# Attention, soft mixture and dense block in one kernel: a weight load moved eight pairs later, diagonals moved ahead of outputs, combining moved to VectorE and partly into the dense stage

## The chip, the cores and the metric

The kernel runs on one core of a Trainium2 chip. The metric is the device time of one execution in microseconds (us), lower is better. The engines are PE (TensorE matmul; PEld is its weight load), DVE (VectorE), ACT (ScalarE), POOL (GpSimd) and SP (SyncE, which here issues every DMA).

## What is computed

Three layers follow each other. The first is linear attention with a decaying state over 4 batches, 8 heads, 768 tokens and 48 dimensions per head. The second is a soft mixture of 8 experts with 4 slots each. The third is a dense block with a gelu between two matrices.

```python
# attention, per batch and head, t = 0..767
y[t] = r[t] @ (state + outer(u * k[t], v[t]))
state = w[t][:, None] * state + outer(k[t], v[t])
# soft mixture: x is (3072, 384), phi (384, 32)
logits = x @ phi
d = softmax(logits, axis=0); slot_input = d.T @ x
slot_out[e] = relu(slot_input[e] @ w1[e]) @ w2[e]      # 8 experts, hidden size 1024
c = softmax(logits, axis=1); x = c @ slot_out
# dense block: w_in (384, 2048), w_out (2048, 384)
h = x @ w_in
out = (h * sigmoid(1.702 * h)) @ w_out
```

`w_in` and `w_out` arrive as 64-bit floats and are turned into 32-bit floats on the chip with integer operations.

## The kernel before, in words

The program has three stages, and the order of the instructions of each engine is the order in which the code is written (`tc.manual_schedule()`).

**The pair loop** (`phase_a`, the loop over `i` at L650). Two heads form a pair, so there are 16 pairs, four to a batch. Iteration `i` works on pair `i` (`cur`), prepares pair `i+1` (`nxt`) and ends pair `i-1` (`prv`). For each pair DVE scans the decays (`products`, L498 and L501), multiplies keys and queries by them (`scale`, L507) and scans the states (L552). ACT makes six diagonal matrices for each half of a pair, `diagonal(i, 0)` and `diagonal(i, 3)` (L534, tile `am`, three buffers). `causal` (L568, DVE) puts PE's scores beside them in `am`. `outputs(i-1, c0)` (PE, L579 and L584) uses `am`, the values `v` and the states, and ends with a copy on ACT to `xt` (L587). `x_tr` (L600) transposes `xt` on PE, ACT copies the result (L601), and `logits` (L811) multiplies `xt` by phi.

The loads go out on SP in the order of the code and wait there until their buffers are free: the decays `z` (L466), keys and queries `rk` (L473), values `v` (L480, two buffers, wanted by `states`, L549, of the next iteration), one 512 KB piece of the first half of `w_in` (L114) in each of the iterations 1 to 6, and one or two 512 KB pieces of the expert weights w1 (L79).

**Combining** (`Batch.combining`, L887). The softmax over the 32 slots of a batch's tokens: DVE subtracts the maximum, ACT takes the exponential, DVE sums and inverts; then ACT multiplies six column groups by the inverse (L901, six instructions) and rounds (L902), DVE takes the rest of the rounding (L908, twice), and POOL copies the rounded half twice (L909). `combined` (L912) transposes the result on PE, three 128x128 blocks for each half of a batch (L917), and ACT copies it to the token buffer `cT`. Batches 0 and 1 are combined in the last iteration, batches 2 and 3 in the expert stage (`phase_b`).

**The expert stage** (`phase_b`). PE multiplies the slot inputs by w1 (L988, four groups of 24), ACT takes the relu (L1009), PE transposes (L1017), DVE copies into `hTm` (L1019, which POOL has set to zero, L999), and PE multiplies by w2 (L1025, 128 instructions). Beside it DVE and ACT turn the six pieces of `w_in` into 32-bit floats (`step`, L290 to L303). Loads of w2 and `w_out` start as each group of L988 frees its buffers (`W.turn`).

**The dense stage** (`phase_c`, loop over `n` at L1235, 96 steps). Each step has one matmul with the combined table (`act`, L1108), a gelu and a rounding on ACT (L1115, L1122), the rest of the rounding on DVE (`low`, L1130, tile `gl`), and nine matmuls (`project`, L1146). Conversions of `w_out` and of the late half of `w_in` run beside it on DVE and ACT. Steps 16 to 23 work on token block 2, steps 24 to 31 on block 3.

Of the kernel before, what the change touches and what calls it, by code (L numbers as in the profile page):

```python
# [27 lines left out]
NS = 32  # L28
# [179 lines left out]
def body(ctx, tc, rkz, z0, vin, vt, wc, uin, phi, w1, w2, w_in, w_out, cst, out):  # L208
# [22 lines left out]
    with ExitStack() as c1:  # L231
        wip = c1.enter_context(tc.tile_pool(name="wip", bufs=1, reuse_waits="tile"))
        ring = c1.enter_context(tc.tile_pool(name="ring", bufs=1, reuse_waits="tile"))
        with tc.manual_schedule(), ExitStack() as c2:
            W = Weights(tc, ring, wip, w1, w2, w_in, w_out)
            short = ExitStack()
            batches, sp, sT = phase_a(tc, rkz, z0, vin, u_sb, prod, ebias, W, c2, short, consts, soft)
            dense = phase_b(tc, W, c2, short, sp, sT, soft, batches, ebias)
            phase_c(tc, W, c2, dense, ebias, soft, out,
                    Check(tc, wc, prod, con, flag, peak))  # L240
# [178 lines left out]
def phase_a(tc, rkz, z0, vin, u_sb, prod, ebias, W, after, late, consts, soft):  # L419
# [5 lines left out]
    with ExitStack() as ctx:  # L425
# [224 lines left out]
        for i in range(n_p + 1):  # L650
# [52 lines left out]
            if cur and i:  # L703
                diagonal(i, 3)
# [8 lines left out]
            if 0 < i <= KT * HF // CV:  # L713
                W.load_in(i - 1)
# [57 lines left out]
class Tokens:  # L772
# [25 lines left out]
class Batch:  # L798
# [88 lines left out]
    def combining(self, room):  # L887

        nc, pool = self.tc.nc, self.pool
        cc, chl = [t.rearrange("p (c s) -> p c s", c=6) for t in halves(room())]  # L890
        mx = pool.tile([128, 6], F32, name="mx", bufs=2)
        nc.vector.tensor_reduce(out=mx, in_=self.l, axis=AX.X, op=ALU.max)
        nc.vector.tensor_tensor(out=cc, in0=self.l, in1=mx.unsqueeze(2).to_broadcast([128, 6, NS]), op=ALU.subtract)
        nc.scalar.activation(cc, cc, AF.Exp)
        yield
        sm = pool.tile([128, 6], F32, name="sm", bufs=2)
        nc.vector.tensor_reduce(out=sm, in_=cc, axis=AX.X, op=ALU.add)
        nc.vector.tensor_scalar_add(sm, sm, 1e-9)
        nc.vector.reciprocal(sm, sm)
        for c in range(6):  # L900
            nc.scalar.mul(cc[:, c], cc[:, c], sm[:, c:c + 1])  # L901
        nc.scalar.copy(chl.bitcast(F32R), cc)  # L902
        yield
        self.c4 = []
        for h in range(2):
            c4 = room().rearrange("p (c a s) -> p c a s", c=3, a=4)
            hi2, cc2 = [t[:, 3 * h:3 * h + 3].unsqueeze(2).to_broadcast([128, 3, 2, NS]) for t in (chl, cc)]
# [14 lines left out]


def halves(t):
    return t[:, 0:6 * NS], t[:, 6 * NS:]
# [9 lines left out]
def phase_b(tc, W, after, late, sp, sT, soft, batches=(), ebias=None):  # L935
# [6 lines left out]
    with late:  # L942
# [9 lines left out]
        step = W.in_steps(ebias, {0: flat, 1: flat, 4: h[:, 512:]}) if batches else lambda *a: None  # L952
# [18 lines left out]
        def combine(b):  # L971
            for bt in batches[b:b + 1]:
                for i in range(2):
                    pct = bt.combined(i, bt.psT.tile())
                    nc.scalar.copy(bt.home(i), pct)

        c2, c3 = [bt.combining(room) for bt in batches[2:]] if batches else (iter(()),) * 2
        next(c2, None)
        step(0, 0)
        step(0, 1)  # L980
        next(c2, None)
        step(0, 2)
        ph = psH.tile([128, 512], F32, name="ps")
        for n, p in enumerate((3, 0, 1, 2)):
# [5 lines left out]
            if n == 0:  # L990
                next(c2, None)
                step(1, 0)
                step(1, 1)
            if n == 1 and batches:
                cT.room(1, F32R)
                combine(2)
                next(c3, None)
                step(1, 2)
                nc.gpsimd.memset(hTm, 0.0)  # L999
                next(c3, None)  # L1000
                step(2, 0)
                step(2, 1)
            W.turn(n)
        next(c3, None)
        step(2, 2)
        if not batches:
            nc.gpsimd.memset(hTm, 0.0)
        for q in range(2):
            nc.scalar.activation(h[:, 256 * q:256 * q + 256], ph[:, 256 * q:256 * q + 256], AF.Relu)  # L1009
        tiny = bp.tile([128, 1], F32, name="tiny")  # L1010
        nc.scalar.activation(tiny, h[:, 0:1], AF.Gelu_apprx_sigmoid)
        combine(3)
# [9 lines left out]
        for e in range(NE):  # L1022
# [11 lines left out]
            for m, i in (((3, 0), (3, 1), (4, 0)), ((4, 1), (3, 2), (5, 0)), ((5, 1), (4, 2)), ((5, 2),))[e] if e < 4 else ():  # L1034
                step(m, i)
# [3 lines left out]
    return cvp, room, psA, mid, psH, psS, po, rep  # L1039


def phase_c(tc, W, after, dense, ebias, soft, out, check=None):
    nc = tc.nc
    con, cT = soft[0], soft[3]
    cvp, room, psA, mid, psH, psS, po, rep = dense
    with ExitStack() as c2:
# [188 lines left out]
        for n in range(1, n_all):  # L1235
# [86 lines left out]
```

## Time and profile before

| | us |
|---|---|
| three runs | 443.34, 444.67, 446.39 |
| median | 444.67 |
| the profiled execution | 444.18 |
| its span, first to last instruction | 442.3 |
| busy in the span: PE, DVE, ACT, POOL | 406.4, 323.0, 265.4, 50.6 |

The mean granted clock of TensorE over the span is 0.967 of full speed. The profile is one execution, recorded by the hardware. A row of a timeline gives the start and the length in us, the engine, the line, the operation and the tiles, and in brackets the idle time just before it and who ended that.

### The profile page before, as it was taken

The page shows a single profiled execution, that of the slowest core. Times are in us where ns is not written, and L with a number is a line of the kernel's source. Part 1 is how long each engine was busy: PE and PEld are TensorE (multiplying, and loading weights), DVE is VectorE, ACT ScalarE, POOL GpSimd, SP SyncE. Part 2 cuts the span into 40 slices and gives each one's busy share as a digit, 9 for nine tenths or more (in the row PEclk, how much of TensorE's full clock was granted, in tenths as well). Part 3 has the DMA queues.
Part 4 walks back from the last instruction along what each step waited for, and adds up shares of the span by engine and source line. Part 5 has one row for each costly group of instructions (what it writes and reads, how often), then busy time and mean ns, then how long its engine had stood idle before and what let it go on. Part 6 is the DMA issues. An engine that isn't in the chain of part 4 may idle for free.

```text
span 442.3 us, 8909 instructions
## 1 busy us (share of the span) xinstructions
PE 406.4 (92%) x3405; PEld 310.7 (70%) x3405; DVE 323.0 (73%) x522; ACT 265.4 (60%) x647; POOL 50.6 (11%) x82
## 2 busy tenths in 40 slices
PE   5887989899999978799999999999999999999993
PEld 1565667667767655295788788877888888888872
DVE  7799599899999755896995888587763765644431
ACT  5476567677777865544875657486565544445530
POOL 4323132222322310220000000000000000000000
PEclk9599699999999998989999999999999999999997
DMA  8969699998785886999500000000000634401102
GB/s 210 225 153 303 182 306 266 243 239 248 192 226 139 317 292 258 368 414 424 240 1 0 0 2 1 1 0 1 18 0 2 185 107 137 142 19 72 71 3 79
DMA packets 24565, 67.35 MB, mean 152 GB/s; under 512 B 2848, under 2 KB 6560, under 8 KB 24256
## 3 DMA queue, kind: packets, MB, share of 16 engines
q1 hardware_dynamic: 24512, 66.67, 48.2%
q8 instruction: 29, 0.48, 0.4%
q14 instruction: 24, 0.20, 0.1%
HBM read 61.94 MB, written 4.72 MB: 151 GB/s over the span
## 4 chain that ended last, share of the span: by engine, by line
PE 65%; DMA 13%; DVE 11%; ACT 5%; issue 2%; POOL 1%; SPq 1%; DVEq 0%; ACTq 0%; POOLq 0%
PE po L1146 43%; DMA v<-in_vin 7%; PE pa L1108 5%; DMA wt<-in_rkz 5%; PE py L584 3%; PE py L579 3%; PE ps L1025 2%; ACT am L534 2%; PE pkv L549 2%; PE pg L562 2%; DMA wt<-in_w_in 2%; DVE wt L498 1%; DVE wt L507 1%; PE ps L600 1%; ACT c L901 1%
## 5 line engine op out<-in xcount | busy, mean ns | idle before, releaser
L1122 ACT CAST gh<-g 128x512 fp32r<-128x512 f32 x96 | 59.4, 619 | 62.5 <-PE po L1146 62.1
L1130 DVE TENSOR_TENSOR gl<-g,gh 128x512 fp32r<-128x512 f32 x96 | 65.2, 687 | 41.8 <-ACT gh L1122 41.4
L1146 PE MATMUL po<-gh,wi 128*128 128x512 f32 x288 | 88.8, 390 | 0.0
L1146 PE MATMUL po<-gh,wt 128*128 128x512 f32 x288 | 83.8, 390 | 0.0
L534 ACT ACTIVATE am<-con,cT 128x128 f32<-128x128 f32 x192 | 59.4, 392 | 9.7 <-DVE cT L527 9.7
L1146 PEld LDWEIGHTS po<-gh,wt 128*128 128x128 f32 x288 | 54.1, 188 | 11.8 <-issue 0.4
L1146 PEld LDWEIGHTS po<-gh,wi 128*128 128x128 f32 x288 | 54.2, 188 | 11.6
L1115 ACT ACTIVATE g<-pa 128x512 f32<-128x512 f32 x96 | 57.0, 594 | 2.5 <-PE pa L1108 1.9
L1146 PE MATMUL po<-gl,wi 128*128 128x512 f32 x144 | 56.4, 391 | 0.0
L1146 PE MATMUL po<-gl,wt 128*128 128x512 f32 x144 | 51.4, 393 | 1.4 <-DVE gl L1130 1.4
L1108 PE MATMUL pa<-cT,wt 128*128 128x512 f32 x96 | 38.4, 402 | 1.1 <-ACT g L1115 1.1
L568 DVE COPY_PREDICATED am<-con,pg 128x768 f32<-128x768 uint32 x32 | 32.3, 1009 | 7.4 <-ACT am L534 7.3
L1146 PEld LDWEIGHTS po<-gl,wt 128*128 128x128 f32 x144 | 27.0, 188 | 7.9 <-DVE gl L1130 2.2
L587 ACT COPY xt<-py 128x384 f32<-128x384 f32 x32 | 15.2, 480 | 28.1 <-PE py L584 27.0
L1146 PEld LDWEIGHTS po<-gl,wi 128*128 128x128 f32 x144 | 27.0, 188 | 5.7
L492 POOL TENSOR_TENSOR rkb<-wt 128x384 f32<-128x384 f32 x25 | 28.0, 1120 | 17.0 <-DMA wt<-in_rkz 11.9
L501 DVE TENSOR_TENSOR_SCAN wt<-wt 128x774 f32<-128x774 f32 x16 | 28.4, 1772 | 0.5
L579 PE MATMUL py<-am,v 128*64 128x128 f32 x384 | 28.4, 283 | 0.4 <-DVE am L568 0.4
L498 DVE TENSOR_TENSOR_SCAN wt<-wt 128x774 f32<-128x774 f32 (+1 forms) x17 | 28.1, 1658 | 0.3 <-DMA wt<-in_z 0.3
L562 PE MATMUL pg<-wt 64*128 64x128 f32 x312 | 25.7, 300 | 0.5 <-DVE am L568 0.5
L562 PEld LDWEIGHTS pg<-wt 64*128 64x128 f32 x312 | 20.6, 197 | 5.7 <-issue 1.8
L579 PEld LDWEIGHTS py<-am,v 128*64 128x64 f32 x384 | 21.1, 140 | 2.7 <-DVE am L568 0.6
(210 smaller groups left out, 581.5 us busy)
## 6 DMA issues: line engine op xcount, KB each, us to landing
wt<-in_w SPq DMA_DIRECT2D x21, 512.0 KB, 7.0
wt<-in_w SPq DMA_DIRECT2D x13, 768.0 KB, 9.2
wt<-in_rkz SPq DMA_DIRECT2D x26, 288.0 KB, 5.2
v<-in_vin SPq DMA_DIRECT2D x16, 296.0 KB, 5.4
c<-in_wc SPq DMA_DIRECT2D x24, 192.0 KB, 2.9
out_dram<-os SPq DMA_DIRECT2D x18, 256.0 KB, 2.1
wt<-in_rkz SPq DMA_DIRECT2D x30, 145.3 KB, 3.9
wi<-in_w_in SPq DMA_DIRECT2D x6, 512.0 KB, 6.4
```

Of the source, the lines that this page charges most:

```text
L492: eng.tensor_tensor(out=rkb[:, c], in0=st[p]["r"][:, c], in1=st[p]["k"][:, c], op=ALU.mult)
L498: nc.vector.tensor_tensor_scan(out=sf[:, o:n][:, ::-1], data0=z[:, o + 1:n + 1][:, ::-1], data1=dS[:, o:n][:, ::-1], initial=0.0, op0=ALU. ...
L501: nc.vector.tensor_tensor_scan(out=x, data0=z[:, 0:XL], data1=dX, initial=0.0, op0=ALU.mult, op1=ALU.add)
L534: nc.scalar.activation(am[:, j, c], ident, AF.Copy, scale=q["coef"][:, c0 + c, j:j + 1])
L562: nc.tensor.matmul(q["pg"][:, j, (c - c0) * CH:(c - c0 + 1) * CH], q["k"][64 * j:64 * j + 64, c * CH:(c + 1) * CH], q["r"][64 * j:64 * j + ...
L568: nc.vector.copy_predicated(q["am", c0], later, q["pg"][:, :, 0:3 * CH].rearrange("p j (c t) -> p j c t", t=CH))
L579: nc.tensor.matmul(py[64 * j:64 * j + 64, (c - c0) * CH:(c - c0 + 1) * CH], q["v"][:, c * 96 + j * 48:c * 96 + j * 48 + 64], q["am", c0][: ...
L1108: nc.tensor.matmul(pa, mst[:, f * 128:(f + 1) * 128], cT.at(tb * 512, 512), start=True, stop=True)
L1115: nc.scalar.activation(g, live[n], AF.Gelu_apprx_sigmoid)
L1122: nc.scalar.copy(gh, live[n])
L1130: nc.vector.tensor_tensor(out=gl, in0=g, in1=gh.bitcast(F32), op=ALU.subtract)
L1146: nc.tensor.matmul(live["po", tb][i], w[:, i * 128:(i + 1) * 128], g, start=(f % FH == 0 and k == 0), stop=(f % FH == FH - 1 and k == 2))
```

## The change

The change has four parts.

1. The six pieces of `w_in` are loaded in the iterations 8 to 13 in place of 1 to 6.
2. `diagonal(i, 3)` stands ahead of `outputs(i-1, 3)` in place of behind it and `scale`.
3. Combining works in place on the tile `l`. The multiplication by the inverse is one DVE instruction per batch, the rounding two on DVE, and POOL copies half as much (L909 copied both halves of a 4-column layout, the new one copies one).
4. For batches 2 and 3 only the subtraction and the exponential stay in the expert stage. The rest runs in the dense stage, on DVE at steps 17 and 25, with the transposes and copies at steps 20 and 28. In the expert stage the conversion has a room of its own for its second piece, the zeros of `hTm` come from ACT in place of POOL, and the load of the gelu's table stands ahead of the conversions in place of behind the relu.

```diff
@@ phase_a, the loop over i
+            if cur and i:
+                diagonal(i, 3)
             if prv:
                 outputs(i - 1, 3)
...
-            if cur and i:
-                diagonal(i, 3)
...
-            if 0 < i <= KT * HF // CV:
-                W.load_in(i - 1)
+            if n_p // 2 <= i < n_p // 2 + KT * HF // CV:
+                W.load_in(i - n_p // 2)
...
             if i == n_p - 1:
-                for _ in range(2):
-                    for it in comb:
-                        next(it, None)
+                for it in comb:
+                    run(it)
@@ combining
-        for c in range(6):
-            nc.scalar.mul(cc[:, c], cc[:, c], sm[:, c:c + 1])
-        nc.scalar.copy(chl.bitcast(F32R), cc)
-        yield
+        nc.vector.tensor_tensor(out=cc, in0=cc, in1=sm.unsqueeze(2).to_broadcast([128, 6, NS]), op=ALU.mult)
...
-            nc.vector.tensor_tensor(out=c4[:, :, 2:], in0=cc2, in1=hi2, op=ALU.subtract)
-            nc.gpsimd.tensor_copy(c4[:, :, 0:2], hi2)
+            part, hi = cc[:, 3 * h:3 * h + 3], c4[:, :, 0]
+            nc.vector.tensor_copy(hi.bitcast(F32R), part)
+            nc.vector.tensor_tensor(out=c4[:, :, 2:], in0=part.unsqueeze(2).to_broadcast([128, 3, 2, NS]),
+                                    in1=hi.unsqueeze(2).to_broadcast([128, 3, 2, NS]), op=ALU.subtract)
+            nc.gpsimd.tensor_copy(c4[:, :, 1], hi)
@@ phase_b
-        step = W.in_steps(ebias, {0: flat, 1: flat, 4: h[:, 512:]}) if batches else lambda *a: None
+        step = W.in_steps(ebias, {0: flat, 1: flat[:, 1024:], 4: h[:, 512:]}) if batches else lambda *a: None
...
+        comb = [bt.combining(room) for bt in batches[2:]]
+        for it in comb:
+            next(it)
+        nc.scalar.activation(bp.tile([128, 1], F32, name="tiny"), con[:, 0:1], AF.Gelu_apprx_sigmoid)
...
             if n == 0:
                 step(1, 2)
                 step(2, 0)
                 step(2, 1)
+                nc.scalar.copy(hTm, con[:, OFF_MASK:OFF_MASK + 1].unsqueeze(2).to_broadcast([128, HT, NE * 36]))
...
-                combine(2)
...
-                nc.gpsimd.memset(hTm, 0.0)
...
-        combine(3)
@@ phase_c, the loop over n
+            for k, (bt, it) in enumerate(zip(batches[2:], comb)):
+                if n == FH * (k + 2) + 1:
+                    run(it)
+                if n == FH * (k + 2) + 4:
+                    for i in range(2):
+                        nc.scalar.copy(bt.home(i), bt.combined(i, bank(1 - k, i)))
             project(n)
```

On ACT in the pair loop, the end of one iteration and the start of the next stand so before. `am` is the tile of the diagonals, `xt` that of the outputs, `xb` that of the transposed outputs.

```order
L514 COPY prod<-wt_80 128x6
L587 COPY xt<-py 128x384 x2
L534 ACTIVATE am<-con,cT_115 128x128 x6
L601 COPY xb<-ps_365 128x288
L601 COPY xb<-ps_370 128x288
```

And so in the changed kernel:

```order
L514 COPY prod<-wt_80 128x6
L587 COPY xt<-py 128x384
L534 ACTIVATE am<-con,cT_115 128x128 x6
L587 COPY xt<-py 128x384
L601 COPY xb<-ps_364 128x288
L601 COPY xb<-ps_369 128x288
```

The six diagonals of the second half moved ahead of the copy of the second outputs. In the last iteration the same copy (of pair 14) also moved behind them.

On ACT in the expert stage, from the exponential of batch 2 to the last conversion, the order before is this. `c` is a combining tile, `hTm`, `wi` and `wt_88` hold conversions, `wt_88<-ps` is the relu.

```order
L894 ACTIVATE c_2350<-c_2350 128x192
L298 ACTIVATE hTm<-hTm,ebias 128x512
L901 ACTIVATE c_2350<-c_2350,sm 128x32 x6
L902 CAST c_2350<-c_2350 128x192
L298 ACTIVATE hTm<-hTm,ebias 128x512
L975 CAST cT_2410<-ps_2411 128x384
L975 CAST cT_2410<-ps_2416 128x384
L894 ACTIVATE c_2421<-c_2421 128x192
L901 ACTIVATE c_2421<-c_2421,sm 128x32 x6
L902 CAST c_2421<-c_2421 128x192
L298 ACTIVATE wi<-wi,ebias 128x512
L1009 ACTIVATE wt_88<-ps 128x256 x2
```

And in the changed kernel:

```order
L892 ACTIVATE l_2009<-l_2009 128x192
L892 ACTIVATE l_2271<-l_2271 128x192
L967 ACT_TABLE_LOAD
L967 ACTIVATE tiny<-con 128x1
L298 ACTIVATE hTm<-hTm,ebias 128x512 x2
L298 ACTIVATE wi<-wi,ebias 128x512
L984 COPY hTm<-con 128x2304
L992 ACTIVATE wt_88<-ps 128x256 x2
```

Fourteen combining instructions (six multiplications and a rounding for each of two batches) and two copies to `cT` left the way to the relu; a table load, which stood behind the relu, and a copy of 2304 columns came onto it. The line numbers here are those of the changed kernel.

On DVE in the dense stage the changed kernel has this at step 17, between the `gl` of steps 18 and 19, which before stood side by side. `l_2009` is the tile of batch 2's exponentials, `c_3042` and `c_3046` its two halves.

```order
L1111 TENSOR_TENSOR gl<-g,gh 128x512
L895 TENSOR_REDUCE sm<-l_2009 128x6
L896 TENSOR_SCALAR sm<-sm 128x6
L897 RECIPROCAL sm<-sm 128x6
L898 TENSOR_TENSOR l_2009<-l_2009,sm 128x192
L903 CAST c_3042<-l_2009 128x3x32
L904 TENSOR_TENSOR c_3042<-l_2009,c_3042 128x3x64
L903 CAST c_3046<-l_2009 128x3x32
L904 TENSOR_TENSOR c_3046<-l_2009,c_3046 128x3x64
L1111 TENSOR_TENSOR gl<-g,gh 128x512
```

Eight instructions of a batch moved from the expert stage to a place between two products that PE waits for; batch 3 has the same at step 25.

## Rows read from the trace of the kernel before

**Rows 1.** Busy us by window: length, PE, PEld, DVE, ACT, POOL, clock, DMA share, GB/s.

```profile
11.40:150.00 138.60, 125.83 (x1800) 92.99 (x1800) 124.53 (x137) 98.95 (x310) 36.86 (x59) 0.94 0.83 228
173.80:190.50 16.70, 13.99 (x113) 5.85 (x114) 14.38 (x32) 10.12 (x29) 3.81 (x5) 0.92 0.95 364
190.50:213.80 23.30, 22.18 (x199) 16.56 (x199) 19.33 (x40) 10.25 (x21) 2.29 (x3) 0.99 1.02 417
213.80:438.00 224.20, 219.47 (x981) 179.01 (x979) 145.36 (x274) 124.89 (x230) 0.00 (x0) 1.00 0.14 47
```

**Rows 2.** The chain that ended last, in the pair loop: start, us, what.

```profile
37.15 7.69 DMA v<-in_vin
44.97 1.04 PE pkv L549 x20
...
59.44 5.50 DMA v<-in_vin
```

**Rows 3.** Two more windows, columns as in the first group.

```profile
45.00:50.00 5.00, 5.00 (x56) 4.30 (x56) 2.40 (x2) 1.16 (x4) 0.18 (x1) 0.50 0.32 73
...
120.00:140.00 20.00, 19.14 (x296) 14.55 (x296) 18.54 (x20) 14.61 (x46) 5.44 (x9) 1.00 0.59 171
```

**Rows 4.** Timeline of DVE, the first scan of three iterations in a row.

```profile
39.25 1.76 DVE L498 TENSOR_TENSOR_SCAN wt<-wt 128x774 f32<-128x774 f32 x1
...
52.42 1.74 DVE L498 TENSOR_TENSOR_SCAN wt<-wt 128x774 f32<-128x774 f32 x1
...
61.18 1.75 DVE L498 TENSOR_TENSOR_SCAN wt<-wt 128x774 f32<-128x774 f32 x1
```

**Rows 5.** Waits between 30 and 150 us: total us, times, longest.

```profile
ACT xt L587 <- PE py L584: 24.9, 13, 6.3
...
DVE am L568 <- ACT am L534: 3.0, 6, 0.6
```

**Rows 6.** Timeline of PE in the last iteration.

```profile
166.40 0.53 PE L811 MATMUL pl<-xt,phis 128*32 128x192 f32 x8 [1.41 <-ACT xt L587]
```

**Rows 7.** Timeline of the expert stage, single engines.

```profile
179.19 0.96 PE L917 MATMUL ps<-con,c 128*128 128x128 f32 x6
...
183.07 2.02 POOL L999 MEMSET hTm<- 128x2304 f32 x1 [3.52 <-DVE wi L303]
...
183.25 1.87 DVE L898 TENSOR_SCALAR sm<-sm 128x6 f32<-128x6 f32 x1
...
188.00 0.64 ACT L1009 ACTIVATE wt<-ps 128x256 f32<-128x256 f32 x2
...
188.12 1.54 PE L917 MATMUL ps<-con,c 128*128 128x128 f32 x6 [2.68 <-POOL c L909]
...
188.66 1.28 ACT L1011 ACT_TABLE_LOAD   x1
...
189.45 1.06 PE L1017 MATMUL ps<-con,wt 128*128 128x128 f32 x4
...
190.47 4.59 PE L1025 MATMUL ps<-wt,hTm 128*32 128x384 f32 x48
```

**Rows 8.** Timeline of the dense stage, DVE and PE around steps 18 to 21.

```profile
253.14 1.28 DVE L1130 TENSOR_TENSOR gl<-g,gh 128x512 fp32r<-128x512 f32 x2
...
256.53 1.28 DVE L1130 TENSOR_TENSOR gl<-g,gh 128x512 fp32r<-128x512 f32 x2
...
256.32 0.39 PE L1146 MATMUL po<-gl,wt 128*128 128x512 f32 x1
...
258.61 0.39 PE L1146 MATMUL po<-gl,wt 128*128 128x512 f32 x1
```

**Rows 9.** Groups of instructions by line, up to 235 us: busy us, mean ns.

```profile
L908 DVE TENSOR_TENSOR c<-c 128x192 f32<-128x192 f32 x6 | 2.3, 428 | 2.6 <-ACT c L902 2.6
...
L909 POOL COPY c<-c 128x192 f32<-128x192 f32 x6 | 2.7, 484 | 27.3 <-ACT c L902 27.3
...
L1122 ACT CAST gh<-g 128x512 fp32r<-128x512 f32 x13 | 8.0, 616 | 2.2 <-PE po L1146 2.0
```

More of the change, by code (lines that the diff above doesn't have):

```diff
@@ L239, in body @@
             phase_c(tc, W, c2, dense, ebias, soft, out,
-                    Check(tc, wc, prod, con, flag, peak))
+                    Check(tc, wc, prod, con, flag, peak), batches)
     ok = nc.values_load(flag, min_val=0, max_val=NFLAG)
@@ L887, in combining @@
     def combining(self, room):
-        nc, pool = self.tc.nc, self.pool
-        cc, chl = [t.rearrange("p (c s) -> p c s", c=6) for t in halves(room())]
+        nc, pool, cc = self.tc.nc, self.pool, self.l
         mx = pool.tile([128, 6], F32, name="mx", bufs=2)
-        nc.vector.tensor_reduce(out=mx, in_=self.l, axis=AX.X, op=ALU.max)
-        nc.vector.tensor_tensor(out=cc, in0=self.l, in1=mx.unsqueeze(2).to_broadcast([128, 6, NS]), op=ALU.subtract)
+        nc.vector.tensor_reduce(out=mx, in_=cc, axis=AX.X, op=ALU.max)
+        nc.vector.tensor_tensor(out=cc, in0=cc, in1=mx.unsqueeze(2).to_broadcast([128, 6, NS]), op=ALU.subtract)
         nc.scalar.activation(cc, cc, AF.Exp)
@@ L906, in combining @@
             c4 = room().rearrange("p (c a s) -> p c a s", c=3, a=4)
-            hi2, cc2 = [t[:, 3 * h:3 * h + 3].unsqueeze(2).to_broadcast([128, 3, 2, NS]) for t in (chl, cc)]
-            nc.vector.tensor_tensor(out=c4[:, :, 2:], in0=cc2, in1=hi2, op=ALU.subtract)
-            nc.gpsimd.tensor_copy(c4[:, :, 0:2], hi2)
+            part, hi = cc[:, 3 * h:3 * h + 3], c4[:, :, 0]
[3 more added lines that the diff above has]
+            nc.gpsimd.tensor_copy(c4[:, :, 1], hi)
             self.c4.append(c4)
@@ L921, in home @@
         return self.soft[3].at(self.b * S + h * 3 * CH, 3 * CH)
-def halves(t):
-    return t[:, 0:6 * NS], t[:, 6 * NS:]
 def slot_inputs(tc, pool, SI):
@@ L969, in room @@
             return sp.tile([128, 12 * NS], F32, name="c4", bufs=3)
[L971 to L978, printed above, removed]
+        comb = [bt.combining(room) for bt in batches[2:]]
+        for it in comb:
+            next(it)
+        nc.scalar.activation(bp.tile([128, 1], F32, name="tiny"), con[:, 0:1], AF.Gelu_apprx_sigmoid)
         step(0, 0)
         step(0, 1)
-        next(c2, None)
+        step(1, 0)
+        step(1, 1)
         step(0, 2)
@@ L990, in phase_b @@
             if n == 0:
[L991 to L995, printed above, removed]
-                combine(2)
-                next(c3, None)
                 step(1, 2)
-                nc.gpsimd.memset(hTm, 0.0)
-                next(c3, None)
                 step(2, 0)
                 step(2, 1)
+                nc.scalar.copy(hTm, con[:, OFF_MASK:OFF_MASK + 1].unsqueeze(2).to_broadcast([128, HT, NE * 36]))
+            if n == 1:
+                step(2, 2)
+                step(3, 0)
+                if batches:
+                    cT.room(1, F32R)
             W.turn(n)
[L1004 to L1007, printed above, removed]
         for q in range(2):
             nc.scalar.activation(h[:, 256 * q:256 * q + 256], ph[:, 256 * q:256 * q + 256], AF.Relu)
-        tiny = bp.tile([128, 1], F32, name="tiny")
-        nc.scalar.activation(tiny, h[:, 0:1], AF.Gelu_apprx_sigmoid)
-        combine(3)
+        step(3, 1)
         h4 = h[:, 0:512].rearrange("p (q c r) -> p q r c", q=2, r=2)
@@ L1033, in phase_b @@
                                           ident.rearrange("p (n s) -> p n s", n=4).unsqueeze(2).to_broadcast([128, 4, 2, NS]))
-            for m, i in (((3, 0), (3, 1), (4, 0)), ((4, 1), (3, 2), (5, 0)), ((5, 1), (4, 2)), ((5, 2),))[e] if e < 4 else ():
+            for m, i in (((3, 2), (4, 0), (4, 1)), ((5, 0), (5, 1), (4, 2)), ((5, 2),))[e] if e < 3 else ():
                 step(m, i)
@@ L1038, in phase_b, with phase_c @@
                 cvp = after.enter_context(tc.tile_pool(name="cvp", bufs=1, side="right", reuse_waits="tile"))
-    return cvp, room, psA, mid, psH, psS, po, rep
-def phase_c(tc, W, after, dense, ebias, soft, out, check=None):
+    return comb, cvp, room, psA, mid, psH, psS, po, rep
+def phase_c(tc, W, after, dense, ebias, soft, out, check=None, batches=()):
     nc = tc.nc
     con, cT = soft[0], soft[3]
-    cvp, room, psA, mid, psH, psS, po, rep = dense
+    comb, cvp, room, psA, mid, psH, psS, po, rep = dense
     with ExitStack() as c2:
```

## The prediction

> **What bounds the kernel now.** I read the busy times by stage first [rows 1]. The reader is to see three regimes. In the pair loop (138.6 us) PE is busy for 125.83 and DVE for 124.53, so both are near their limit and the time is lost in short waits. In the expert stage (16.7 us) PE has 13.99 and DVE 14.38, and the DMA share is 0.95. In the dense stage PE is busy for 219.47 of 224.20, so every matmul added there costs its full length, and DVE has slack (145.36).
>
> Then I read the chain of waits. In the pair loop one link stands out: the values `v` issued at 37.15 land 7.69 us later, and `states` on PE starts only then, at 44.97 [rows 2]. The next such link takes 5.50. After the wait PE runs at half its clock: the granted clock is 0.50 between 45 and 50 us [rows 3], which is its level of 1.2 GHz. On DVE the first scan of this iteration (iteration 3) stands at 39.25, that of the next at 52.42, the one after at 61.18 [rows 4]. So iteration 3 takes 13.17 us and the next one 8.76.
>
> Then the waits by engine. ACT waits 24.9 us in 13 waits for the second outputs of the pair before, and DVE waits 3.0 us in 6 waits for the diagonals that stand behind that wait on ACT [rows 5]. In the expert stage PE waits 2.68 us for POOL's copy of batch 3's combining weights before it may transpose them, and only behind these does it transpose the relu and start on w2 at 190.47 [rows 7].
>
> All terms are set against the profiled execution, 444.18 us: its span of 442.3 and 1.9 around it. The median of the three runs is 0.5 above it, and I leave that out.
>
> **Part 1, `w_in` eight pairs later.** Six loads of 512 KB move; none is added. When the slow `v` is issued, two of the six are ahead of it or right behind it on SP. Without them its 7.69 us should fall to about the 5.50 of the next link or below, and 2.2 us is most of the wait; the half clock after the wait goes with it. So iteration 3 should take what iteration 4 took, 8.76, although that one had its own piece of `w_in`: 13.17 - 8.76 = 4.4 gained. What is late next is again `v`: its buffer comes free at the end of an iteration, and 5.5 us of landing and the 20 matmuls of `states` follow, which fills the 8.76 us. So nothing below that is to be had from this part.
>
> The pieces now meet iterations 8 to 13, queued behind `v` and ahead of w1, as before. Their price there has two ends. It is nothing where the DMA has room: between 120 and 140 us (iterations 12 and 13) its share is 0.59 [rows 3]. It is 4.4 us for one stall like that of iteration 3. I take 0.5, near the lower end, because iteration 4 shows what a piece costs without the backlog of the start: 8.76 us, no stall. Net of part 1: -3.9.
>
> **Part 2, diagonals ahead of outputs.** On ACT six diagonals now fill the wait for the second outputs, 24.9 / 13 = 1.9 us on average [rows 5]. At most DVE's 3.0 us are gained. The other end is a loss: where ACT comes late, the copy to `xt` slips behind the diagonals, and PE's transposes, which read it, wait. No row shows this; with a slip of 0.5 us in three iterations it is +1.5. I take -1.2, less than half of the 3.0, since in most iterations the `v` link sets the pace [rows 2] and takes back what DVE gains.
>
> In the last iteration the multiplications and roundings of two batches (14 instructions) leave ACT, and with them the wait of 1.41 us that PE has there for the copy of `xt` [rows 6]. Against it, `x_tr` of pair 14 now waits for a copy that stands behind the diagonals, and DVE has six instructions more. Between -1.4 and +0.5 I take -1.2, near the row: PE has other work queued in both orders, and DVE's work is done before the next maximum is asked for.
>
> **Part 3, the expert stage.** PE loses six transposes ahead of its third group, 0.96 us, the wait of 2.68, and six transposes from 188.12 to the relu's transposes at 189.45, 1.33 [rows 7]. The relu, 0.64, lay beside that wait and is now on the path. That is 0.96 + 2.68 + 1.33 - 0.64 = 4.3, and I take 4.0 for new gaps. Its cover is ACT: the zeros for `hTm` stand ahead of the relu. They take between 2.0 us (POOL's time for the same columns [rows 7]) and 2.8 (4.5 times a 512-column rounding of 616 ns [rows 9]). DVE needs 14 instructions before ACT may start on them, at 14.38 / 32 = 0.45 each 6.3 us [rows 1], so until about 180; with a conversion between, ACT is done near 184. PE's first layer ends at 185.44 - 0.96 = 184.5 (before, it ended 2.68 ahead of 188.12). So the zeros just fit. DVE, relieved of ten small instructions and of the 1.87 us below, should have its conversions done before PE is through w2.
>
> One instruction of six columns on DVE took 1.87 us, and it lies within POOL's zeroing of `hTm`, 183.07 to 185.09 [rows 7]. The Trainium skill (SBUF — State Buffer, "Who interferes with whom") says that GpSimd and a VectorE copy, cast or scalar operation in a two-port mode take turns at one shared port pair, each for the whole instruction; the trace agrees. That rule also speaks against the change, which puts two casts per batch on DVE beside POOL's copies; it is a rival below.
>
> The gelu's table load took 1.28 us [rows 7]. It now stands ahead of the first conversion on ACT, where DVE still has four subtractions and the first half of a conversion to do; it costs nothing. The Trainium skill (ScalarE: Activation LUTs, "Rules for kernel authors") budgets about 2.7 us for a switch to another set; by that the zeros would end some 1.4 us later, and the sum would be 438.2 in place of 436.8. The row decides.
>
> **Part 4, the dense stage.** Twelve transposes come to PE. At full clock six took 0.96 us, after the wait 1.54 [rows 7]; between 1.9 and 3.1 for twelve, and I take 1.9, since the clock here is 1.00 [rows 1]. On DVE eight instructions come between two `gl`. The dearest kind took 428 ns [rows 9], so at most 3.4 us per batch; most handle fewer columns, and I take 2.4. The `gl` of step 19 is ready at 254.42 and wanted at 256.32, that of step 20 ready near 257.2 and wanted at 258.61 [rows 8]: 1.9 and 1.4 us of slack. Step 19 becomes 2.4 - 1.9 = 0.5 late. Step 20 is then wanted 0.5 later, and 0.96 more by the transposes ahead of it, so it waits for nothing. That is 0.5 per batch, 1.0 for both; the ends are nothing and 2 x (3.4 - 1.4) = 4.0. ACT's four copies lie in its idle time (124.89 busy of 224.20). Part 4: +2.9.
>
> **Sum.** -3.9 - 1.2 - 1.2 - 4.0 + 2.9 = -7.4, so 444.18 - 7.4 = 436.8.
>
> **Rivals.**
>
> *The stall moves.* `v` of one of the iterations 8 to 11 lands late, because these have all other loads too. For it: the DMA share over the loop is 0.83 [rows 1]. Against it: iteration 4 had a piece and no stall. One stall of 4.4 gives 441.2.
>
> *Loads hold the second layer.* PE comes to w2 four us earlier, but the loads that start with the first layer do not come earlier, and the DMA share is 0.95 and then 1.02 [rows 1]. The price is up to the 4.0 of part 3; half of it gives 438.8.
>
> *The diagonals bring nothing.* The copy of `xt` takes over as what PE waits for. That gives 436.8 + 1.2 = 438.0.
>
> *POOL's copies hold DVE.* A copy of twice the columns took 484 ns [rows 9]; four copies in the dense stage, each holding DVE once, are up to 1.9 us on PE's path, 438.7. This is the port rule of the Trainium skill named above (SBUF — State Buffer).
>
> *Slower.* The loads of iterations 8 to 11 (keys, queries, decays, values, one or two pieces of w1 and now one of `w_in`) fill the queue so that `v` stalls in each as in iteration 3, with the half clock behind it. Four stalls are 17.6 us: 454.4. From three on (436.8 + 13.2 = 450.0) the change is slower by over 1%. Against it stand the iterations 1, 2 and 4 to 6 of before, which had the same loads, and one stall among six.
>
> *More is gained.* All 3.0 us of the diagonals and nothing lost in the later iterations give 436.8 - 1.8 - 0.5 = 434.5, and less with PE at full clock in the second layer.
>
> **How the numbers follow.** A measurement of this kernel can tell about 1% from no change, 4.4 us of the median of 444.67. The forecast (434 to 440) has 0.52, the moved stall 0.17, the held second layer 0.10, idle diagonals 0.06, POOL's copies 0.04, the slower case 0.05, the larger gain 0.06. Faster by over 1% means below 440.2: the forecast but for its upper edge (0.48), the four smaller rivals (0.10 + 0.06 + 0.04 + 0.06), 0.74. Within 1%: the moved stall and that edge, 0.21. Slower: 0.05. The range reaches from 432.5 (the larger gain with two us to spare) to 441.5 (the moved stall), and leaves out the slower case and the tails.
>
> **What would show it.** Right: iteration 3 takes about 8.8 us between scans and the clock stays at 1.00 there; DVE's waits for the diagonals in the pair loop fall from 3.0 us to under 1; the first matmul on w2 comes about 4 us sooner after the first of the first layer; the dense stage from its first step grows by about 3 us. Wrong: waits of PE for `v` in iterations 8 to 11; PE waiting for the copy of `xt` at the transposes; PE waiting for w2 loads or for the zeros; a wait for `gl` of over 1 us at steps 18 to 21 or 26 to 29.

## The result, and the profile after

The changed kernel takes 431.75 us (median of four runs, 430.79 to 432.31) against 444.96 for the kernel before on the same chip: ratio 0.9736, 95% interval 0.9694 to 0.9779. That is faster by 2.6%, 11.7 us by the ratio and 13.2 by the medians, where 7.4 was forecast. The median lies 0.75 us below the range of the prediction; by the ratio on the prediction's 444.67 it is 432.9, just inside. The sign was right, and so was that of every stage that had a term; the gain was larger than the terms.

The two profiled executions are compared by stage. The bounds are the first scan of iterations 1 and 14 (DVE L498), the first matmul of the first layer (L988 before, L978 after), of the second (L1025, now L1006) and of the first `project` (L1146, now L1127).

| stage | before | after | change | forecast |
|---|---|---|---|---|
| start to iteration 1 | 22.42 | 20.95 | -1.47 | 0 |
| iterations 1 to 13 | 120.10 | 114.47 | -5.63 | -5.1 |
| iteration 14 to the first layer | 31.30 | 27.97 | -3.33 | -1.2 |
| first layer to the second | 16.65 | 11.92 | -4.73 | -4.0 |
| second layer to `project` | 19.90 | 19.63 | -0.27 | 0 |
| `project` to the end of the span | 231.93 | 234.06 | +2.13 | +2.9 |
| span | 442.3 | 429.0 | -13.30 | -7.4 |

Busy times in the five stages from iteration 1 on, after the change (columns as in [rows 1]):

```profile
20.90:135.40 114.50, 106.27 (x1621) 79.71 (x1622) 108.94 (x122) 87.65 (x270) 29.12 (x51) 1.00 0.87 238
135.40:163.40 28.00, 24.54 (x409) 18.52 (x409) 19.83 (x46) 18.87 (x61) 6.04 (x8) 1.00 0.89 320
163.40:175.30 11.90, 11.28 (x100) 4.19 (x100) 11.06 (x25) 8.16 (x13) 0.00 (x0) 1.00 1.03 400
175.30:194.90 19.60, 19.02 (x185) 14.11 (x188) 14.49 (x30) 6.74 (x14) 2.24 (x3) 1.00 1.04 417
194.90:429.00 234.10, 224.14 (x1003) 182.00 (x1001) 152.82 (x297) 128.46 (x238) 1.63 (x4) 0.99 0.17 59
```

From iteration 1 up to the dense stage the clock is 1.00, which it was not before [rows 1, 3]. In the first layer PE is now busy for 11.28 of 11.90 us.

The scans that answer to [rows 4], and the links of the chain that answer to [rows 2], both after:

```profile
29.02 1.76 DVE L498 TENSOR_TENSOR_SCAN wt<-wt 128x774 f32<-128x774 f32 x1
37.15 1.75 DVE L498 TENSOR_TENSOR_SCAN wt<-wt 128x774 f32<-128x774 f32 x1
46.19 1.75 DVE L498 TENSOR_TENSOR_SCAN wt<-wt 128x774 f32<-128x774 f32 x1
```

```profile
35.76 5.54 DMA v<-in_vin
41.43 0.66 PE pkv L549 x20
44.47 5.32 DMA v<-in_vin
```

Iteration 3 takes 46.19 - 37.15 = 9.04 us in place of 13.17; `v` lands in 5.54 in place of 7.69, and `states` takes 0.66 behind it, at full clock, in place of 1.04. Iterations 8 to 13, where the pieces now are, take 53.55 us together against 53.08.

In the last iteration, the expert stage and the dense stage, the timeline of single engines after (these answer to [rows 6 to 8]):

```profile
152.65 0.55 PE L600 MATMUL ps<-con,xt 128*128 128x128 f32 x3 [1.81 <-ACT xt L587]
...
156.65 0.55 PE L914 MATMUL pg<-con,c 128*128 128x128 f32 x3
...
157.48 0.51 PE L810 MATMUL pl<-xt,phis 128*32 128x192 f32 x8
...
171.29 2.10 ACT L984 COPY hTm<-con 128x2304 f32<-128x2304 f32 x1
173.98 0.66 ACT L992 ACTIVATE wt<-ps 128x256 f32<-128x256 f32 x2 [0.59 <-PE ps L978]
...
174.42 0.78 PE L998 MATMUL ps<-con,wt 128*128 128x128 f32 x4 [0.52 <-ACT wt L992]
...
241.44 0.50 PE L1127 MATMUL po<-gl,wt 128*128 128x512 f32 x1 [0.38 <-DVE gl L1111]
...
243.41 0.82 PE L914 MATMUL po<-con,c 128*128 128x128 f32 x6
```

Both waits of the old last iteration are gone: that for POOL's copy ahead of the first combining transposes (1.42 us before) and that for the copy of pair 15's outputs ahead of `logits` [rows 6]. A new one of 1.81 us stands ahead of pair 14's transposes. In the expert stage ACT ends its zeros at 173.39 and then waits 0.59 us for PE. In the dense stage PE waits 0.38 us for the product of step 19.

### The profile page after: what moved, and what is told of

The parts are those of the page before. It is cut to its first block, busy times and chain, and to the rows that moved or that the text cites. A ratio compares the mean times of both kernels' runs of the same rounds, so it can differ in the third digit from the quotient of the medians.

```text
span 429.0 us, 8870 instructions
## 1 busy us (share of the span) xinstructions
PE 399.3 (93%) x3402; PEld 305.5 (71%) x3405; DVE 323.5 (75%) x534; ACT 261.3 (61%) x620; POOL 48.4 (11%) x81
## 4 chain that ended last, share of the span: by engine, by line
PE 70%; DMA 11%; DVE 8%; ACT 4%; issue 2%; SPq 1%; POOL 1%; DVEq 0%; ACTq 0%; POOLq 0%
PE po L1127 43%; DMA v<-in_vin 9%; PE pa L1089 5%; PE py L584 3%; PE py L579 3%; PE ps L1006 3%; PE ps L978 2%; DMA wt<-in_rkz 2%; PE pkv L549 2%; PE pg L562 2%; ACT am L534 2%; SPq L473 1%; PE ps L600 1%; DVE gl L1111 1%; PE ps L280 1%
## 5 line engine op out<-in xcount | busy, mean ns | idle before, releaser
L1127 PE MATMUL po<-gh,wi 128*128 128x512 f32 x288 | 88.9, 390 | 0.0
L1127 PE MATMUL po<-gh,wt 128*128 128x512 f32 x288 | 84.0, 391 | 0.0
L1127 PEld LDWEIGHTS po<-gh,wi 128*128 128x128 f32 x288 | 54.2, 188 | 11.6
L1127 PEld LDWEIGHTS po<-gh,wt 128*128 128x128 f32 x288 | 54.0, 188 | 11.6 <-issue 0.4
L1127 PE MATMUL po<-gl,wi 128*128 128x512 f32 x144 | 56.4, 391 | 0.0
L1127 PE MATMUL po<-gl,wt 128*128 128x512 f32 x144 | 51.6, 395 | 1.8 <-DVE gl L1111 1.7
L1127 PEld LDWEIGHTS po<-gl,wt 128*128 128x128 f32 x144 | 27.0, 188 | 9.2 <-DVE gl L1111 3.5
L1127 PEld LDWEIGHTS po<-gl,wi 128*128 128x128 f32 x144 | 27.0, 188 | 5.7
L498 DVE TENSOR_TENSOR_SCAN wt<-wt 128x774 f32<-128x774 f32 (+1 forms) x17 | 28.1, 1655 | 0.2 <-DMA wt<-in_z 0.2
L601 ACT COPY xb<-ps 128x288 f32<-128x288 f32 x28 | 11.2, 399 | 22.8 <-PE ps L600 22.8
L1147 DVE TENSOR_TENSOR os<-po,wt 128x512 f32<-128x512 f32 x18 | 12.4, 692 | 13.7 <-PE po L1127 13.7
```

The source lines that it names most:

```text
L498: nc.vector.tensor_tensor_scan(out=sf[:, o:n][:, ::-1], data0=z[:, o + 1:n + 1][:, ::-1], data1=dS[:, o:n][:, ::-1], initial=0.0, op0=ALU. ...
L1127: nc.tensor.matmul(live["po", tb][i], w[:, i * 128:(i + 1) * 128], g, start=(f % FH == 0 and k == 0), stop=(f % FH == FH - 1 and k == 2))
```

## The experiments

The kernel before was run again beside each group of four: medians of 443.83, 444.72 and 442.19 us. Within a few us the comparison by stage is therefore sharper than the times. Two stages scatter between profiles whatever the kernel: the start to iteration 1 (20.00 to 23.63 us over all profiles) and the loop (112.62 to 115.86 over the eight that share the changed kernel's loop). So the 1.47 us of the start in the first table are not the change's.

### The loads and the diagonals, each alone

b_win is the kernel before with the first edit, b_diag the kernel before with the second, a_win and a_diag the changed kernel with one or the other undone.

```diff
-            if 0 < i <= KT * HF // CV:
-                W.load_in(i - 1)
+            if n_p // 2 <= i < n_p // 2 + KT * HF // CV:
+                W.load_in(i - n_p // 2)
```

```diff
+            if cur and i:
+                diagonal(i, 3)
             if prv:
                 outputs(i - 1, 3)
...
-            if cur and i:
-                diagonal(i, 3)
```

Expected of b_win: 

> The kernel before with part 1 alone (the six pieces of w_in in iterations 8 to 13). In the changed kernel the first scan of iteration 14 starts 7.1 us earlier (142.52 to 135.42), 4.1 of it in iteration 3. Theory: these 4.1 us are the loads', and the rest of the loop's gain is not. So the stall of iteration 3 is gone (about 9 us between its scans in place of 13.17, clock 1.00 from 45 to 50 us) and the time falls by 3.5 to 4.5 us, to about 440.7. Rival: the diagonals took the stall away, since they decide when PE frees the buffer of v: then iteration 3 stays near 13 us here and the time within 1 us of before.

Expected of b_diag: 

> The kernel before with part 2 alone (the second diagonals ahead of the second outputs). Theory: it takes 2 to 3 us from the loop, spread over the iterations (ACT's wait of 24.9 us for the outputs falls to about 4), the stall of iteration 3 stays (12 to 13 us between its scans), and in the last iteration it costs up to 1.8 us, PE's wait for the copy of the outputs of pair 14. The time falls by 0.5 to 2.5 us. Rival: the diagonals carry the loop's whole gain, 6 us or more, to about 438.5, and iteration 3 takes 9 us.

Expected of a_win: 

> The changed kernel with part 1 undone (w_in back in iterations 1 to 6). Theory: 3.5 to 4.5 us slower than the changed kernel, about 435.8, nearly all of it in one iteration between 2 and 5, with PE at half its clock behind the wait. Rival (the diagonals took the stall): within 1 us of the changed kernel's 431.75.

Expected of a_diag: 

> The changed kernel with part 2 undone (second diagonals behind the second outputs and the scaling). Theory: the iterations are 2 to 3 us longer in sum, the last iteration up to 1.8 shorter, so 0.5 to 2.5 us slower than the changed kernel, about 433.3, and iteration 3 stays near 9 us. Rival: 436 or more, with the stall of iteration 3 back.

Measured: b_win 438.58 us (ratio to before 0.9885, interval 0.9809 to 0.9960), b_diag 442.73 (0.9969, 0.9931 to 1.0007), a_win 438.77 (0.9890, 0.9854 to 0.9927), a_diag 433.37 (0.9813, 0.9755 to 0.9872).

| loop, iterations 1 to 13 | loads early | loads late |
|---|---|---|
| diagonals behind the outputs | 120.10 (before) | 115.29 (b_win) |
| diagonals ahead | 120.19 (b_diag), 119.79 (a_win) | 114.47 (after) |

a_diag is a second profile of the upper right cell, 115.23. The loads carry the loop: 4.8 us without the diagonals, 5.3 with them. By this table the diagonals bring nothing with early loads, where 2 to 3 us were expected of b_diag, and 0.8 with late ones, which is inside the scatter of the loop.

All profiles together say more. In the four with the diagonals behind (before, b_win, a_diag, b_warm) iteration 2 takes 8.74 to 8.84 us and iterations 6 to 13 together 71.7 to 72.4. In the ten with the diagonals ahead iteration 2 takes 8.10 to 8.37, and iterations 6 to 13 take 70.6 to 71.4 in nine and 73.2 in a_best_warm. So outside iterations 3 to 5 the diagonals save about 1.5 us, with early loads too. Over the whole loop with late loads the mean of the eight is 114.1 us against 115.3 of the two (b_win, a_diag), 1.1 less; the profiles overlap, so the size is not settled. ACT's wait mostly moves on: that for the second outputs falls from 23.9 us to 3.4 (both from 30 to 140 us), and that for the transposes behind them (L601) grows from 5.3 to 19.6.

Why the loop of b_diag is no shorter is in its chain and its windows:

```profile
38.24 7.17 DMA v<-in_vin
...
50.12 5.29 DMA v<-in_vin
...
58.59 7.32 DMA v<-in_vin
```

```profile
45.00:50.00 5.00, 4.45 (x56) 3.65 (x56) 2.41 (x2) 1.05 (x3) 0.18 (x1) 0.66 0.44 136
65.00:70.00 5.00, 3.94 (x48) 3.25 (x50) 2.67 (x3) 1.42 (x6) 0.53 (x2) 0.66 0.68 233
```

There are two slow landings now, each with a stretch of low clock behind it: iteration 3 takes 11.99 us and iteration 5 12.30 (9.37 before). a_win has the same two, 12.38 and 12.25. In the kernels with late loads neither stands. The second slow landing takes back what the other iterations gained: iterations 3 to 5 last 32.78 us together in place of 31.30. That the second comes because shorter iterations ask for `v` sooner than early loads allow is argued, not shown; that it needs the early loads and the diagonals ahead is shown.

a_diag is 1.6 us slower than the changed kernel, and the intervals of the two ratios overlap. a_win is 7.0 us slower, where 3.5 to 4.5 were expected, and more than the 5.3 of the loop. 1.46 us of the rest lie in the last iteration: after the same wait of 1.81 us its clock falls to 0.50 from 162 to 164 us, where that of the changed kernel stays at 1.00.

In the last iteration b_diag shows something that the first table hides: with all fourteen instructions still on ACT the stage takes 29.50 us in place of 31.30. Its timeline of PE:

```profile
161.10 0.55 PE L600 MATMUL ps<-con,xt 128*128 128x128 f32 x3 [1.86 <-ACT xt L587]
...
166.58 0.55 PE L917 MATMUL pg<-con,c 128*128 128x128 f32 x3
...
167.41 0.51 PE L811 MATMUL pl<-xt,phis 128*32 128x192 f32 x8
```

The order of the diagonals puts a wait of 1.86 us ahead of the transposes of pair 14, and the two waits behind it (1.42 and 1.41 before) are gone, although the clock is 0.50 from 162.5 to 165 us. a_diag, which has the new combining and not this order, takes 27.94 us, as long as the changed kernel. So the gains of the two edits in the last iteration overlap and cannot be added. The stage also scatters where the clock falls: b_win, which has it in common with the kernel before, takes 32.30.

### The clock in the last iteration and the expert stage

```diff
+        keep_warm(nc, pg[:, 0], con[:, 0:320].bitcast(BF16), 8)
         evac = [(bat[1], 0, bat[1].combined(0, pg[:, 0]))]
         next(fill)
         next(fill)
+        keep_warm(nc, pg[:, 1], con[:, 0:320].bitcast(BF16), 8)
         logits(n_p - 1)
```

(and twelve ahead of batch 3's transposes; the logits here are those of pair 15, which the expectation calls pair 14)

Expected of b_warm: 

> The kernel before, with matmuls on constants that nothing reads put on PE just ahead of its three long waits behind the pair loop: eight ahead of the first combining transposes (1.42 us of wait), eight ahead of the logits of pair 14 (1.41), twelve ahead of batch 3's transposes (2.68). No work of the program moves. In the kernel before the clock is 0.50 from about 167 to 171 us and from 188 to 191.5, in the changed kernel it is 1.00 there. Theory: the half clock is a loss of its own, about 2 us in the first stretch and 1 in the second, and it is what my terms for the last iteration (-1.2 forecast, -3.3 seen) left out. Then this is 1.5 to 3 us faster than before, with the clock at 1.00 in both stretches. Rival: the stretches are filled by waits that end when they end, clock or no clock; then within 0.7 us of before.

Measured: 441.86 us against 444.72 (ratio 0.9955, interval 0.9915 to 0.9994). The windows of the kernel before and of b_warm:

```profile
167.50:170.00 2.50, 2.50 (x25) 1.79 (x25) 0.50 (x3) 0.87 (x3) 0.82 (x1) 0.50 1.03 410
170.00:172.50 2.50, 2.50 (x78) 2.19 (x76) 1.05 (x4) 1.25 (x6) 0.00 (x0) 0.88 0.17 68
187.50:190.00 2.50, 1.88 (x9) 1.88 (x10) 2.21 (x4) 2.47 (x5) 0.89 (x2) 0.54 1.03 415
```

```profile
167.50:170.00 2.50, 2.50 (x86) 2.15 (x90) 1.28 (x5) 1.05 (x6) 0.46 (x1) 1.00 0.68 274
170.00:172.50 2.50, 1.63 (x31) 0.81 (x23) 1.75 (x8) 2.38 (x8) 0.00 (x0) 1.00 0.39 64
187.50:190.00 2.50, 2.25 (x27) 2.12 (x31) 2.47 (x10) 1.95 (x6) 0.31 (x1) 1.00 1.02 412
```

The clock stays at 1.00 and the stages are shorter by 0.92 us (31.30 to 30.38) and 0.53 (16.65 to 16.12), though no work moved and 28 idle matmuls were added. So the half clock (1.2 GHz) was a loss of its own, 1.5 us by this pair of profiles, half of what the theory allowed at most.

### Combining in the last iteration on ACT

```diff
-        nc.vector.tensor_tensor(out=cc, in0=cc, in1=sm.unsqueeze(2).to_broadcast([128, 6, NS]), op=ALU.mult)
+        for c in range(6):
+            if self.b < 2:
+                nc.scalar.mul(cc[:, c], cc[:, c], sm[:, c:c + 1])
...
```

Expected of a_mul: 

> The changed kernel with the multiplication by the inverse for batches 0 and 1 back on ACT, six instructions for each batch (the rounding stays on DVE). Theory: ACT's twelve instructions, 2.8 us in the kernel before, again hold the copies of the last outputs and POOL's copies; PE waits 1.4 to 2.8 us more in the last iteration, and if its clock falls behind that, 1.5 us more: 1.4 to 4.5 us slower than the changed kernel. Rival: that stage got shorter by other things (the order of the diagonals), and ACT has room: within 0.7 us.

Measured: 434.15 us, 2.4 slower than the changed kernel; its stage takes 30.18 us against 27.97. One wait holds the difference, in PE's timeline:

```profile
161.37 0.53 PE L810 MATMUL pl<-xt,phis 128*32 128x192 f32 x8 [2.00 <-ACT xt L587]
```

ACT's two groups of six took 1.38 us each and stood ahead of the copies of the last outputs, as in the kernel before. The clock did not fall behind this wait.

### Batches 2 and 3 finished in the expert stage

```diff
+        if batches:
+            run(comb[0])
         step(0, 0)
...
                     cT.room(1, F32R)
+                    combine(2)
+            if n == 2 and batches:
+                run(comb[1])
...
+        combine(3)
         step(3, 1)
```

(`combine` makes the transposes and copies of a batch, as in the kernel before; the two places in the dense stage are taken out)

Expected of a_expert: 

> The changed kernel with part 4 undone: batches 2 and 3 are finished in the expert stage, on DVE (batch 2 ahead of the conversions, batch 3 behind the third group, transposes and copies as in the kernel before). Dense stage: about 2.1 us shorter (234.1 back to 231.9). Theory A: the expert stage gives back all that it had gained, 4.7 us, as DVE is full there and PE waits for batch 3 again: net 2 to 3 us slower than the changed kernel. Theory B: taking ACT's six multiplications and roundings out was most of the gain, and only the twelve transposes (about 2 us) come back: net within 0.7 us.

Measured: 435.52 us, 3.8 slower than the changed kernel. The dense stage is 2.8 us shorter (231.25), the first layer to the second 5.65 longer (17.57), and the second layer 1.0 longer, with the clock at 0.50 from 180 to 182.5 us, where it starts. PE's and DVE's timelines at the place:

```profile
178.94 1.28 PE L914 MATMUL ps<-con,c 128*128 128x128 f32 x6 [4.03 <-DVE c L903]
```

```profile
176.90 0.35 DVE L895 TENSOR_REDUCE sm<-l 128x6 f32<-128x192 f32 x1
...
178.95 0.36 DVE L904 TENSOR_TENSOR c<-l,c 128x192 f32<-128x192 f32 x1
```

Theory A holds, with more than its price (5.65 us given back where it says 4.7): batch 3's part starts only when DVE is through its conversions, at 176.90, and PE waits 4.03 us for it. Taking the work off ACT was not the gain in this stage (17.57 with it on DVE, 16.65 with it on ACT and POOL before); taking it out of the stage was. This holds for DVE's order here; batch 3's part ahead of the conversions was not tried.

### The start of combining behind the last outputs

```diff
-            if i == n_p - 1:
...
-                for it in comb:
-                    next(it)
...
             if cur and i:
                 diagonal(i, 3)
             if prv:
                 outputs(i - 1, 3)
+            if i == n_p - 1:
...
+                for it in comb:
+                    next(it)
```

Expected of a_late: 

> The changed kernel with the start of batches 0 and 1's combining (two maxima, subtractions and exponentials) moved behind the second outputs of the last iteration, so that ACT's diagonals and the copy of pair 14's outputs no longer stand behind the exponentials. Theory: PE's wait of 1.81 us for that copy goes, 1 to 1.8 us faster than the changed kernel. Rival: with the diagonals undone in the run before this, that wait was gone and the stage was as long as with it (27.93 and 27.97 us), so DVE or the combining takes over: within 0.7 us.

Measured: 429.43 us (428.36 to 430.31), below every run of the changed kernel; ratio to before 0.9657 (0.9592 to 0.9722). The stage takes 25.94 us against 27.97, and the wait of 1.81 is gone, in PE's timeline and by the window:

```profile
151.96 0.87 PE L600 MATMUL ps<-con,xt 128*128 128x128 f32 x6
```

```profile
137.05:163.00 25.95, 24.31 (x407) 18.50 (x407) 19.75 (x46) 18.65 (x61) 6.09 (x8) 1.00 0.96 339
```

PE is busy for 24.31 of 25.95 us there (24.54 of 28.00 in the changed kernel). The rival falls: undoing the diagonals only exchanged one wait for others (in a_diag PE is idle for 3.1 us of the stage, in the changed kernel for 3.5, in a_late for 1.6), moving the exponentials behind them removed it.

### Zeros on POOL, the dense work divided, and the combinations

a_zero puts the zeros of `hTm` on POOL, a_split divides DVE's eight instructions over two steps (up to the multiplication in the first), a_best is a_late with a_split, a_best_warm adds idle matmuls at the start.

```diff
-                nc.scalar.copy(hTm, con[:, OFF_MASK:OFF_MASK + 1].unsqueeze(2).to_broadcast([128, HT, NE * 36]))
+                nc.gpsimd.memset(hTm, 0.0)
```

```diff
+        if self.b > 1:
+            yield
...
                 if n == FH * (k + 2) + 1:
-                    run(it)
+                    next(it)
+                if n == FH * (k + 2) + 2:
+                    run(it)
```

Expected of a_zero: 

> The changed kernel with the zeros for the tile hTm on POOL again in place of ACT, at the same place in the order. On ACT they took 2.10 us and ended 0.59 us before the relu could start. Theory: they cost nothing on either engine: within 0.7 us of the changed kernel, though a DVE conversion beside POOL's zeroing may be up to 1.9 us longer, since DVE is no longer what PE waits for in that stage. Rival: DVE is held as in the kernel before (1.87 us in one instruction), its copies into hTm come late and the second layer starts 1 to 2 us later.

Expected of a_split: 

> The changed kernel with DVE's eight instructions of a batch in the dense stage divided over two steps, four at steps 17 and 25, four at 18 and 26. In the changed kernel PE waits 0.38 us for the product at step 18 and its next matmul is slowed, and nothing is seen at step 26; my term was 1.0 us. Theory: 0.4 to 0.6 us faster than the changed kernel, less than this measurement can tell, and visible only as that wait gone and the dense stage that much shorter (234.06 us). Rival: the wait moves by one step and stays.

Expected of a_best: 

> The changed kernel with the start of the combining of batches 0 and 1 behind the second outputs (which alone gave 429.4 against 431.75) and the division of the dense-stage work over two steps, both together. Theory: they add, as they lie in different stages: 428.5 to 429.5, the stage from the first scan of iteration 14 to the first layer near 25.9 us. Rival: the gain of the first was the chip's spread; then 431 or more.

Expected of a_best_warm: 

> The same, with more matmuls on constants that nothing reads in PE's waits before and in iteration 0 (17 in place of 12 at the start, four ahead of the first transposes of the keys, five ahead of the first states). In every run so far the clock was 0.50 for 5 to 10 us between 10 and 21 us, and iteration 0 took from 8.70 us (where that was shortest) to 11.03. Theory: the clock stays at 1.00 there, and iteration 0 takes about 8.7 us: 1 to 2 us faster than without. Rival: iteration 0 waits for loads and for ACT's twelve diagonals, and the extra matmuls only stand in the way: no faster, or up to 1 us slower.

Measured: a_zero 431.68 us, a_split 430.38, a_best 429.16 (427.71 to 429.96; ratio to before 0.9710, interval 0.9646 to 0.9774), a_best_warm 429.67.

a_zero's time cannot be told from the changed kernel's, but its stage can: 13.25 us against 11.92. The rival holds there. DVE, POOL and PE:

```profile
169.38 2.32 DVE L291 TENSOR_SCALAR wi<-wi 128x512 int32<-128x512 int32 x1
```

```profile
169.25 2.17 POOL L984 MEMSET hTm<- 128x2304 f32 x1 [10.68 <-PE ps L978]
```

```profile
175.47 1.93 PE L1006 MATMUL ps<-wt,hTm 128*32 128x384 f32 x18 [1.43 <-DVE hTm L1000]
```

In the changed kernel the same instruction takes 0.42 us (at 170.55). Beside POOL's zeroing, 169.25 to 171.42, it took 2.32, to 171.70; DVE's copies into `hTm` began 12.98 us behind the layer's first matmul in place of 11.64, and PE waited 1.43. This is the rule that the prediction took from the Trainium skill (SBUF — State Buffer, "Who interferes with whom"), and the trace agrees. In both kernels a later L291 takes 1.25 us beside another zeroing on POOL (177.23, beside 177.24 to 178.21, in the changed one).

a_split: the wait of 0.38 us (its expectation calls the step 18, it is project's step 19) is gone and the dense stage takes 233.39 us against 234.06, 0.7 less, where 0.4 to 0.6 was expected; the time alone would not show it. a_best has both gains, 25.93 us and 233.21, and they add; it is the fastest kernel of the study by its median, 2.6 us below the changed one. It cannot be told from a_late by the times, and by the ratio a_late is ahead. In a_best_warm the clock is 1.00 from 10 to 20 us, and iteration 0 takes 9.97 us, against 10.22 in a_best, so it is no faster than the scatter of the start can show. The rival holds in the time; its reason, the loads and the diagonals, was not shown. Iteration 0 took 8.60 in a_zero and 8.70 in a_diag, whose start was not edited. In these two the clock was at 0.50 for some 3.4 us, less than the 5 to 10 that the expectation gives for every run. As 1.00 throughout gave 9.97, the clock alone does not set the iteration, and what does was not settled.

## Why the prediction was right, and where it was short

**Part 1 (-4.4, then +0.5).** Right in mechanism and near in size. Iteration 3 took 9.04 us where 8.76 was forecast (8.78 in b_win), at full clock. Of the two pieces that the argument names, the one ahead shows. The loads land there in the order of issue: before, the piece issued at 28.46 landed at 34.92, the two of w1 behind it at 38.20 and 40.96, `v` at 44.84, and the piece right behind `v` at 47.05. In b_win the two of w1, issued as early, landed at 35.20 and 38.36. The later iterations took 0.47 more, which the profiles cannot tell from nothing (52.8 to 55.4 with late loads). The loop gained 4.8 to 5.3 us by this part, where the terms say 3.9. What the argument missed is that the part protects a second place: once the diagonals make the iterations shorter, iteration 5 stalls as well with early loads. "Iteration 4 shows what a piece costs" rested on a loop that was slow enough.

**Part 2, the loop (-1.2).** Near in size with late loads, but not settled: 0.8 us by one pair of profiles, 1.1 by the means. DVE's wait for the diagonals went as forecast, from 3.0 us to none between 30 and 140 us. Only part of ACT's wait for the outputs could be filled, since its next wait took most of it over. With early loads nothing is left in the loop's length (120.10 and 120.19); there it is the `v` link of iteration 5 that takes the gain back, and not the copy of `xt`, which the rival "the diagonals bring nothing" names.

**Part 2, the last iteration (-1.2).** This term was mis-sized most: -3.33 was measured. It counted one of two waits. The other stood in PE's timeline of the kernel before, and I passed over it:

```profile
163.97 0.55 PE L917 MATMUL pg<-con,c 128*128 128x128 f32 x3 [1.42 <-POOL c L909]
```

This wait for POOL's copy ahead of the first combining transposes hung on the same fourteen instructions of ACT. The half clock behind both was left out too. The multiplications are worth 2.2 us in the changed kernel (a_mul) and the clock 0.9 in the kernel before (b_warm). These are no division of the 3.33, since the order of the diagonals alone took 1.8 off the stage (b_diag); what each edit's share is stays open. The cost side was low too: the copy of pair 14 slipped not by 0.5 us but by a wait of 1.81, and a_late shows that this was 2.0 us still to be had.

**Part 3 (-4.0).** -4.73 and then -0.27. The sum of 4.3 holds; the 0.3 held back for new gaps was not needed, and the transposes at half clock had also slowed what followed (0.53 by b_warm). The zeros fitted, with 0.59 us to spare, and left on POOL they would have cost 1.33. The gelu's table took 1.28 us (165.23 to 166.51) and hid, as ACT waited 2.71 us for DVE behind the conversions that followed.

**Part 4 (+2.9).** +2.13. DVE's insertion cost what was forecast: step 19 is 0.67 us longer than the 2.28 of its neighbours and step 27 0.36, 1.0 in sum. The transposes lengthen their steps by 0.68 each, 1.4 in place of 1.9: the six cost less beside the matmuls around them than the 0.96 that their row shows. The rest is scatter.

**The rivals.** The stall did not move and the slower case did not come: no iteration from 8 to 13 takes more than 9.56 us, and the longest landing of `v` is 6.0. The loads did not hold the second layer, although the DMA share is 1.04 there: it runs from 175.31 as it did from 190.47. POOL's copies did not hold DVE: beside them its casts take 0.24 to 0.25 us, so the hold that the rival priced does not show for these copies.

So the forecast missed 5.9 us of the profile's 13.3: 2.1 in the last iteration, 1.5 in the start, which is scatter, and 0.5, 0.7, 0.3 and 0.8 in the other stages, in the order of the table.

## What to carry to other kernels

When instructions leave an in-order engine, list every wait of the other engines that hangs on them, not the largest alone, and ask what the clock did behind each: the stage of the last iteration gained 3.3 us where one wait of 1.41 had been counted. Two edits on one loop need the four corners: here one alone shortened most iterations and lost it again to a stall that only the other removes. What is most worth moving out of a full stage is what the next stage does not need yet, and work put at the head of an in-order engine's queue should be asked who waits for the entry behind it.

## What was not expected of the hardware

A wait of 1.81 us on PE at the same place was followed by the half clock in a_win (0.50 from 162 to 164 us) and not in the changed kernel, nor was one of 2.00 us in a_mul; the rows do not show why. And keeping the clock at 1.00 from 10 to 20 us bought nothing that the scatter of the start would show, while the same at 167 to 171 us bought 0.9. That PE was not what the start waited for would fit, and is not shown.
